# Batch 0 by pairs of heads instead of halves of heads and of slots, in a linear attention followed by two matrix products with a gelu

## Chip, cores and metric

The kernel runs on one core of a Trainium2 chip (trn2). The metric is the device time in microseconds (us) of one execution; the median of five runs counts. The profile is of one execution, and times in it run from its start.

## What is computed

Eight batches of eight heads, 576 positions, 64 elements a head. The attention is linear (no softmax), and its output goes through two matrix products with a gelu between them:

```python
def phi(x, c, s):
    r = np.maximum(x, 0.0)
    return np.concatenate([r * c, r * s], axis=-1)
q_p = phi(q, cos_w, sin_w)
k_p = phi(k, cos_w, sin_w)
kv = np.einsum('bhsf,bhsd->bhfd', k_p, v)
z = np.sum(k_p, axis=2)
num = np.einsum('bhsf,bhfd->bhsd', q_p, kv)
den = np.einsum('bhsf,bhf->bhs', q_p, z)[..., None] + 1e-06
x = num / den                      # then (B*S, H*D) = (4608, 512)
h = x @ w_in                       # w_in 512 x 2048
out = (h * (1.0 / (1.0 + np.exp(-1.702 * h)))) @ w_out    # w_out 2048 x 512
```

The sum z is had from the same matmul as kv: v has a 65th column of ones, so a numerator matmul gives 64 elements of the numerator and the denominator beside them.

## The kernel before

**Tiles.** The 4608 tokens are taken in nine blocks of 512. The first product (`mm1`, L289) gives a block's hidden values in 16 slices of 128 rows: each is four matmuls, one for each row group of 128 of x (`KC` = 4), over 512 columns, and a gelu on ScalarE (L286). The second (`mm2`, L315) multiplies them by w_out, four tiles of 128 tokens, 16 matmuls each. Batch b+1's attention is woven into block b by a table of slots (`at`, L485): what stands at slot n is issued behind slice n of the block.

**Batch 0** has nothing to hide behind and is written out by hand (L356 to L478). Its 512 first positions are four column groups ("slots") of 128; the tail of 64 positions comes later, in slot 13 of block 0 (L490). The steps, all in bf16 with f32 in PSUM:

- `prep` (L199): relu times cosine and relu times sine, for q and k, four heads at a time. Each is one instruction, on VectorE or ScalarE as `on` says.
- `turn_q0` (L360): transposes of q on TensorE, with a copy to `qT` on ScalarE, four of them.
- `kv0` (L367): k^T v, six matmuls a head, and a cast to `kvs` on ScalarE.
- `num0` (L378): eight numerator matmuls into an `at` tile: half of the heads (n) and two slots (p).
- `inv0`, `product0` (L389, L397): denominator plus eps, reciprocal, and numerator times reciprocal into `xb`, on VectorE. A group can be done slot by slot.
- `turn_x0` (L402): transposes of `xb` into a free part of the same `at` tile, and a copy into `xT` on ScalarE. A group covers two row groups (`2 * n` and the next) and two slots.
- `mm1_first` (L413): the first four slices of the first product (`first`, four PSUM tiles), in column pieces of 128, 128 and 256, as the slots come in.

**What sets the order.** The schedule is by hand: each engine does its instructions in the order of the program text, and waits by semaphores. There are two `at` tiles (two PSUM banks each) and four `mm` tiles, given out in turn, and a new user waits until the last reader of the tile is done. `warmup` (L72) issues matmuls on zeros between steps. The loads are in the order of L119 to L144, nearly all on GpSimd's queue: q and k and v of batch 0, w_in, w_out with batch 1 between, then batch 2. The tail of q of batch 0 is turned by a transposing DMA on SyncE's queue (`turn_q`, L218, called at L478), as q of batches 2 and later is.

The order of the stretch in question, cut:

```python
    kv0(kv_lo, 0, 4)
    kv0(kv_hi, 4, 6)
    na0 = num0(0, 0)
    kv0(kv_hi, 6, 8)
    product0(na0, inv0(na0), 0, 0)
...
    first = [mm_tile() for _ in range(4)]
    K4 = (0, 1, 2, 3)
    mm1_first(0, K4, 0, 128)
    turn_x0(nb0, 1, 0, (1, 2))
...
    for fc in range(4):
        mm1_first(fc, (2, 3), 256, 512)
        gelu(first[fc], fc)
```

Of the kernel before, what the change touches and what calls it, by code (L numbers as in the profile page):

```python
# [9 lines left out]
F32 = mybir.dt.float32  # L10
BF16 = mybir.dt.bfloat16
# [10 lines left out]
def kernel(  # L22
# [9 lines left out]
    nc = tc.nc  # L32
# [322 lines left out]

    prep_new(0)  # L356
    s0 = state[0]
    nums = {}
# [8 lines left out]
    def kv0(kv, h0, h1):  # L367

        v3 = s0["v"][:96].rearrange("p (j d) -> p j d", d=D)
        for h in range(h0, h1):  # L370
            for c in range(6):
                j = h * 6 + c
                nc.tensor.matmul(kv[:, ts(h % 4, 128)].rearrange("p (j d) -> p j d", j=2), kp[:96, c, h, :],  # L373
                                 v3[:, j:49:48 - j, :], start=(c == 0), stop=(c == 5))
        nc.scalar.copy(s0["kvs"][:, h0 // 4, h0 % 4:h0 % 4 + h1 - h0, 0:D + 1],
                       kv.rearrange("p (h e) -> p h e", e=128)[:, h0 % 4:h0 % 4 + h1 - h0, 0:D + 1])

    def num0(n, p):  # L378
        nm = at_tile()
        for s in range(2):  # L380
            for h in range(4):
                nc.tensor.matmul(nm[:, s, ds(h * (D + 1), D + 1)], qT[:, 4 * n + h, ts(2 * p + s, 128)],
                                 s0["kvs"][:, n, h, 0:D + 1], start=True, stop=True)
        return nm

    def nm4(nm, s0_, s1):
        return nm[:, s0_:s1, 0:4 * (D + 1)].rearrange("p s (h e) -> p s h e", e=D + 1)

    def inv0(nm, s=(0, 2)):  # L389
        k = s[1] - s[0]  # L390
        den = two.tile([128, 8], F32, name="den").rearrange("p (s h) -> p s h", s=2)[:, 0:k]
        inv = two.tile([128, 8], F32, name="inv").rearrange("p (s h) -> p s h", s=2)[:, 0:k]
        nc.vector.tensor_scalar(den, nm4(nm, *s)[:, :, :, D], 1e-6, None, op0=ADD)
        nc.vector.reciprocal(inv, den)
        return inv

    def product0(nm, inv, n, p, s=(0, 2)):  # L397
        k = s[1] - s[0]
        nc.vector.tensor_tensor(s0["xb"][:, 2 * p + s[0]:2 * p + s[1], 4 * n:4 * n + 4, :], nm4(nm, *s)[:, :, :, 0:D],
                                inv.unsqueeze(3).to_broadcast([128, k, 4, D]), op=MUL)  # L400

    def turn_x0(nm, n, p, s=(0, 2)):  # L402

        w = nm.rearrange("p b e -> p (b e)").bitcast(BF16).rearrange("p (b e) -> p b e", b=2)[:, :, 768:1024]
        for c in range(*s):
            for j in range(2):
                nc.tensor.transpose(w[:, c, ts(j, 128)], s0["xb"][:, 2 * p + c, 4 * n + 2 * j:4 * n + 2 * j + 2, :]
                                    .rearrange("p h d -> p (h d)"), ident)
        nc.scalar.copy(xT[:, 2 * n:2 * n + 2, (2 * p + s[0]) * 128:(2 * p + s[1]) * 128]  # L409
                       .rearrange("p j (s t) -> p s j t", t=128),  # L410
                       w[:, s[0]:s[1]].rearrange("p s (j t) -> p s j t", j=2))

    def mm1_first(fc, kcs, c0, c1):  # L413
        for kc in kcs:
            nc.tensor.matmul(first[fc][:, c0:c1], w_in_sb[:, kc, ts(fc, 128)], xT[:, kc, c0:c1],  # L415
                             start=(kc == 0), stop=(kc == KC - 1))
# [9 lines left out]
    prep_q0(0, 0, (VE, AC))  # L426
    prep_q0(0, 1, (VE, AC))
    for n, p in ((0, 0), (0, 1), (1, 0), (1, 1)):
        if n:
            prep_q0(n, p)  # L430
        turn_q0(n, p, AC.copy)
        if (n, p) != (1, 1):
            warmup(2)
    for n in range(2):
        for c in range(6):
            prep(0, "k", c, 4 * n, 4 * n + 4, on=(VE, AC if c > 2 else VE))
    idle = mm_tile()
    warmup(11, idle)
    kv_lo, kv_hi = mm_tile(), mm_tile()
    kv0(kv_lo, 0, 4)  # L440
    kv0(kv_hi, 4, 6)
    na0 = num0(0, 0)
    kv0(kv_hi, 6, 8)
    product0(na0, inv0(na0), 0, 0)
    warmup(2, idle)
    nb0 = num0(1, 0)
    turn_x0(na0, 0, 0)
    inv = inv0(nb0, (0, 1))
    product0(nb0, inv, 1, 0, (0, 1))
    inv = inv0(nb0, (1, 2))  # L450
    warmup(2, idle)
    na1 = num0(0, 1)
    warmup(1, idle)
    turn_x0(nb0, 1, 0, (0, 1))
    product0(nb0, inv, 1, 0, (1, 2))
    product0(na1, inv0(na1), 0, 1)
    warmup(2, idle)
    first = [mm_tile() for _ in range(4)]
    K4 = (0, 1, 2, 3)
    mm1_first(0, K4, 0, 128)  # L460
    turn_x0(nb0, 1, 0, (1, 2))
    for fc in (1, 2, 3):
        mm1_first(fc, K4, 0, 128)
    for fc in (0, 1):
        mm1_first(fc, K4, 128, 256)
    nb1 = num0(1, 1)
    turn_x0(na1, 0, 1)
    product0(nb1, inv0(nb1), 1, 1)
    for fc in (2, 3):
        mm1_first(fc, K4, 128, 256)  # L470
    for fc in range(4):
        mm1_first(fc, (0, 1), 256, 512)
    turn_x0(nb1, 1, 1)
    for fc in range(4):
        mm1_first(fc, (2, 3), 256, 512)
        gelu(first[fc], fc)
# [92 lines left out]
```

## Time and profile before

| | |
|---|---|
| median of five runs | 299.13 us (298.83 to 299.15) |
| the profiled execution: time | 299.13 us |
| its span | 297.2 us |
| instructions | 5124 |
| granted TensorE clock | 1.00 over the span |
| DMA | 39.65 MB, mean 133 GB/s |

How to read what follows. PE is TensorE's matmuls, PEld its weight loads, DVE is VectorE, ACT ScalarE, POOL GpSimd, SP SyncE. A line of a timeline has start, duration, engine, line of the kernel, operation, output and inputs, shapes and the number of instructions merged, and in brackets the idle time of the engine before it and what ended it. A line of the waits has the waiting engine and line, what it waited for, and the sum, the number and the longest of these waits. A matmul's duration holds its latency; the spacing of starts tells what it takes of TensorE.

### The profile page before, as it was taken

To read this page: it belongs to the slowest core of one execution; us is meant where nothing else is said; L and a number is where in the kernel's file an instruction comes from. 1 tells how busy PE (TensorE), PEld (TensorE's weight loads), DVE (VectorE), ACT (ScalarE), POOL (GpSimd) and SP (SyncE) were. 2 spreads that over 40 slices of the span, in tenths; PEclk is the share of its full clock that TensorE was granted. 3 is DMA by queue.
4 is the path that set the end of the run, shared out by engine and by line. 5 is a ranking of instruction groups with operands and counts; after the bars stand their busy time and mean duration, and the time that the engine had idled before them with its cause. 6 is when DMAs were issued, how large, how long until landed. Compare 5 with 4: busy or idle time off the path is not lost.

```text
span 297.2 us, 5124 instructions
## 1 busy us (share of the span) xinstructions
PE 285.8 (96%) x1956; PEld 146.8 (49%) x1992; DVE 106.1 (36%) x358; ACT 125.9 (42%) x214; POOL 97.6 (33%) x117
## 2 busy tenths in 40 slices
PE   8998999999799999999999999999999999999994
PEld 3674456555344554455445544554455444444443
DVE  5760455773490158114811482148214200000000
ACT  7827542672126512651175116511751167127411
POOL 8542270620259015800690159004501200120021
PEclk9999999999999999999999999999999999999999
DMA  7999999999979977995699969996902510011033
GB/s 188 191 204 176 201 199 193 194 137 173 187 145 175 186 115 136 184 192 99 118 186 147 166 134 185 146 156 124 187 2 60 121 42 1 35 73 35 0 70 71
DMA packets 87303, 39.65 MB, mean 133 GB/s; under 512 B 57136, under 2 KB 85040, under 8 KB 87280
## 3 DMA queue, kind: packets, MB, share of 16 engines
q0 software_dynamic: 40848, 27.01, 60.2%
q1 hardware_dynamic: 46272, 12.20, 26.3%
q8 instruction: 15, 0.25, 0.3%
q10 hardware_dynamic: 160, 0.13, 0.2%
q14 instruction: 8, 0.07, 0.1%
HBM read 36.70 MB, written 9.44 MB: 155 GB/s over the span
## 4 chain that ended last, share of the span: by engine, by line
PE 87%; DMA 5%; DVE 3%; ACT 2%; issue 1%; ACTq 0%; DVEq 0%
PE mm L281 39%; PE mm L321 37%; DMA qT<-qn 4%; PE at L265 3%; PE at L244 3%; DMA q<-in_q_dram 1%; PE mm L345 1%; DVE qn L207 1%; PE mm L415 1%; ACT g L286 1%; PE mm L373 1%; PE mm L75 1%; ACT xT L409 1%; DVE xb L273 1%; ACT qT L226 1%
## 5 line engine op out<-in xcount | busy, mean ns | idle before, releaser
L321 PE MATMUL mm<-w_out_sb,g 128*128 128x512 bf16 x543 | 126.4, 379 | 0.6
L281 PE MATMUL mm<-xT,w_in_sb 128*128 128x512 bf16 x547 | 122.7, 377 | 0.9
L333 POOL DMA_DIRECT2D out_dram<-ysb x54 | 50.6, 942 | 174.6 <-ACT ysb L331 173.1
L286 ACT ACTIVATE g<-mm 128x512 bf16<-128x512 f32 x144 | 85.6, 598 | 45.9 <-PE mm L281 44.9
L281 PEld LDWEIGHTS <-w_in_sb 128*128 128x128 bf16 x564 | 54.3, 98 | 64.1 <-issue 0.2
L321 PEld LDWEIGHTS <-g 128*128 128x128 bf16 x560 | 52.2, 98 | 57.0
L331 ACT COPY ysb<-mm 128x512 f32<-128x512 f32 x34 | 19.9, 586 | 99.8 <-PE mm L321 99.8
L248 DVE CAST kvs<-at 128x260 bf16<-128x260 f32 x14 | 5.4, 426 | 59.3 <-PE at L244 59.3
L273 DVE TENSOR_TENSOR xb<-at,inv 128x512 bf16<-128x512 f32 (+1 forms) x36 | 24.8, 689 | 1.2
L271 DVE TENSOR_SCALAR den<-at 128x8 f32<-128x8 f32 (+1 forms) x36 | 5.9, 164 | 46.0 <-PE at L265 46.0
L350 DVE COPY ysb<-mm 128x256 f32<-128x256 f32 x1 | 0.4, 425 | 59.4 <-PE mm L345 59.4
L265 PEld LDWEIGHTS <-qT 128*128 128x128 bf16 x272 | 12.9, 98 | 10.4 <-DMA qT<-qn 2.5
L207 DVE TENSOR_SCALAR qn<-q,cosw 128x512 bf16<-128x512 bf16 (+1 forms) x36 | 12.4, 349 | 12.1 <-DMA q<-in_q_dram 12.1
L265 PE MATMUL at<-kvs,qT 128*128 128x65 bf16 x272 | 14.2, 194 | 2.5 <-DMA qT<-qn 2.0
L207 DVE TENSOR_SCALAR qn<-q,sinw 128x512 bf16<-128x512 bf16 (+1 forms) x34 | 13.1, 384 | 0.0
L244 PEld LDWEIGHTS <-kp 128*128 128x128 bf16 (+1 forms) x288 | 9.6, 97 | 1.7
L244 PE MATMUL at<-vt,kp 128*128 128x65 bf16 (+1 forms) x288 | 9.8, 193 | 0.0
L86 POOL DMA_DIRECT2D v<-in_v_dram x10 | 8.3, 833 | 2.2 <-DMA w_in_sb<-in_moe_w_in_dram 2.2
L95 POOL DMA_DIRECT2D kt<-in_k_dram x6 | 8.2, 1362 | 1.9 <-DMA k<-in_k_dram 1.9
L86 POOL DMA_DIRECT2D k<-in_k_dram x9 | 7.8, 863 | 2.6 <-ACT g L286 1.9
L207 DVE TENSOR_SCALAR kp<-k,cosw 128x512 bf16<-128x512 bf16 x24 | 8.4, 350 | 0.0
L207 DVE TENSOR_SCALAR kp<-k,sinw 128x512 bf16<-128x512 bf16 x24 | 8.1, 338 | 0.0
(75 smaller groups left out, 141.8 us busy)
## 6 DMA issues: line engine op xcount, KB each, us to landing
out_dram<-ysb POOLq DMA_DIRECT2D x38, 128.0 KB, 3.0
out_dram<-ysb POOLq DMA_DIRECT2D x16, 256.0 KB, 3.0
q<-in_q_dram POOLq DMA_DIRECT2D x7, 512.0 KB, 10.4
k<-in_k_dram POOLq DMA_DIRECT2D x6, 512.0 KB, 12.0
v<-in_v_dram POOLq DMA_DIRECT2D x6, 512.0 KB, 13.0
w_out_sb<-in_moe_w_out_dram POOLq DMA_DIRECT2D x4, 512.0 KB, 19.0
w_in_sb<-in_moe_w_in_dram POOLq DMA_DIRECT2D x3, 512.0 KB, 11.9
q<-in_q_dram SPq DMA_DIRECT2D x2, 512.0 KB, 4.2
```

What stands on the lines that cost most here:

```text
L86: on.dma_start(out=state[b][n][:np_, t * D * h0:t * D * h1].rearrange("p (h e) -> p h e", h=h1 - h0), in_=SRC[n][b, h0:h1, 0:np_ * t, :].r ...
L95: on.dma_start(out=t.rearrange("p (h d) -> p h d", h=H), in_=SRC[n][b, :, 512:576, :].rearrange("h p d -> p h d"))
L207: nc.vector.tensor_scalar(oc, i, 0.0, wc, op0=MAX, op1=MUL)
L244: nc.tensor.matmul(kv[:, ds(h % 4 * (D + 1), D + 1)], kp[:r, c, h, :], vt[:r, c, h, 0:D + 1], start=(c == 0), stop=(c == last))
L265: nc.tensor.matmul(nm[:, h // 4, ds(h % 4 * (D + 1), D + 1)], q_slot(b, c)[:, h, :], state[b]["kvs"][:, h // 4, h % 4, 0:D + 1], start=Tru ...
L271: nc.vector.tensor_scalar(den[:r], nm4[:, :, :, D], 1e-6, None, op0=ADD)
L273: nc.vector.tensor_tensor(state[b]["xb"][:r, c].rearrange("p (n h) d -> p n h d", n=2), nm4[:, :, :, 0:D], inv[:r].unsqueeze(3).to_broadca ...
L281: nc.tensor.matmul(hps[:, c0:c1], w_in_sb[:, kc, ds(fc * 128, 128)], xT[:, kc, ds(i * TB + c0, c1 - c0)], start=(kc == 0), stop=(kc == KC ...
L286: nc.scalar.activation(g, hps, AF.Gelu_apprx_sigmoid)
L321: nc.tensor.matmul(yps, gT[fc][:, ds(t * 128, 128)], w_out_sb[:, fc, :], start=(fc == 0), stop=(fc == FC - 1))
L331: nc.scalar.copy(ysb, cur[t])
L333: nc.gpsimd.dma_start(out=out[row:row + (n - 1) * step + 1:step, :], in_=ysb[p0:p0 + n, :])
```

## The change

Batch 0 is done by pairs of heads (m from 0 to 3) from k^T v on. A pair is one row group of x. `kv0(m)` makes k^T v of one pair in an `mm` tile of its own, with a cast for each pair (four casts, before three). `num0(m)` makes the numerators of a pair over all four slots, eight matmuls in one `at` tile. `product0(m)` has one denominator, one reciprocal and one multiply of 512 elements a pair: four products, before five. `turn_x0(m)` does four transposes and one copy of 512 contiguous elements into `xT`'s row group m: four copies, before five. `mm1_first(kc, *fcs)` has 512-column matmuls: 16 of them, before 32 of 128 columns and 16 of 256. So the first product goes row group by row group instead of column group by column group. Four warmup matmuls fewer stand in the stretch (14 against 18 from the eleven on).

Besides, the sine part of one q relu (half 1, first pair of slots) goes from VectorE to ScalarE, whose three such relus now stand ahead of the four `qT` copies, and the sine part of one k relu goes from ScalarE to VectorE. On POOL's and SP's queues nothing is added, removed or moved.

```diff
-    def kv0(kv, h0, h1):
-
+    def kv0(m):
+
+        kv = mm_tile()
         v3 = s0["v"][:96].rearrange("p (j d) -> p j d", d=D)
-        for h in range(h0, h1):
+        for h in (2 * m, 2 * m + 1):
             for c in range(6):
                 j = h * 6 + c
-                nc.tensor.matmul(kv[:, ts(h % 4, 128)].rearrange("p (j d) -> p j d", j=2), kp[:96, c, h, :],
+                nc.tensor.matmul(kv[:, ts(h % 2, 128)].rearrange("p (j d) -> p j d", j=2), kp[:96, c, h, :],
                                  v3[:, j:49:48 - j, :], start=(c == 0), stop=(c == 5))
-        nc.scalar.copy(s0["kvs"][:, h0 // 4, h0 % 4:h0 % 4 + h1 - h0, 0:D + 1],
-                       kv.rearrange("p (h e) -> p h e", e=128)[:, h0 % 4:h0 % 4 + h1 - h0, 0:D + 1])
-
-    def num0(n, p):
-        nm = at_tile()
-        for s in range(2):
-            for h in range(4):
-                nc.tensor.matmul(nm[:, s, ds(h * (D + 1), D + 1)], qT[:, 4 * n + h, ts(2 * p + s, 128)],
-                                 s0["kvs"][:, n, h, 0:D + 1], start=True, stop=True)
-        return nm
-
-    def nm4(nm, s0_, s1):
-        return nm[:, s0_:s1, 0:4 * (D + 1)].rearrange("p s (h e) -> p s h e", e=D + 1)
-
-    def inv0(nm, s=(0, 2)):
-        k = s[1] - s[0]
-        den = two.tile([128, 8], F32, name="den").rearrange("p (s h) -> p s h", s=2)[:, 0:k]
-        inv = two.tile([128, 8], F32, name="inv").rearrange("p (s h) -> p s h", s=2)[:, 0:k]
-        nc.vector.tensor_scalar(den, nm4(nm, *s)[:, :, :, D], 1e-6, None, op0=ADD)
+        o = 2 * m % 4
+        nc.scalar.copy(s0["kvs"][:, m // 2, o:o + 2, 0:D + 1], kv[:, 0:256].rearrange("p (h e) -> p h e", e=128)[:, :, 0:D + 1])
+
+    def num0(m):
+
+        nms[m] = at_tile().rearrange("p b e -> p (b e)").rearrange("p (s e) -> p s e", s=4)
+        for s in range(4):
+            for h in range(2):
+                nc.tensor.matmul(nms[m][:, s, ds(h * (D + 1), D + 1)], qT[:, 2 * m + h, ts(s, 128)],
+                                 s0["kvs"][:, m // 2, 2 * m % 4 + h, 0:D + 1], start=True, stop=True)
+
+    def product0(m):
+        nm4 = nms[m][:, :, 0:2 * (D + 1)].rearrange("p s (h e) -> p s h e", e=D + 1)
+        den = two.tile([128, 8], F32, name="den").rearrange("p (s h) -> p s h", s=4)
+        inv = two.tile([128, 8], F32, name="inv").rearrange("p (s h) -> p s h", s=4)
+        nc.vector.tensor_scalar(den, nm4[:, :, :, D], 1e-6, None, op0=ADD)
         nc.vector.reciprocal(inv, den)
-        return inv
-
-    def product0(nm, inv, n, p, s=(0, 2)):
-        k = s[1] - s[0]
-        nc.vector.tensor_tensor(s0["xb"][:, 2 * p + s[0]:2 * p + s[1], 4 * n:4 * n + 4, :], nm4(nm, *s)[:, :, :, 0:D],
-                                inv.unsqueeze(3).to_broadcast([128, k, 4, D]), op=MUL)
-
-    def turn_x0(nm, n, p, s=(0, 2)):
-
-        w = nm.rearrange("p b e -> p (b e)").bitcast(BF16).rearrange("p (b e) -> p b e", b=2)[:, :, 768:1024]
-        for c in range(*s):
-            for j in range(2):
-                nc.tensor.transpose(w[:, c, ts(j, 128)], s0["xb"][:, 2 * p + c, 4 * n + 2 * j:4 * n + 2 * j + 2, :]
-                                    .rearrange("p h d -> p (h d)"), ident)
-        nc.scalar.copy(xT[:, 2 * n:2 * n + 2, (2 * p + s[0]) * 128:(2 * p + s[1]) * 128]
-                       .rearrange("p j (s t) -> p s j t", t=128),
-                       w[:, s[0]:s[1]].rearrange("p s (j t) -> p s j t", j=2))
-
-    def mm1_first(fc, kcs, c0, c1):
-        for kc in kcs:
-            nc.tensor.matmul(first[fc][:, c0:c1], w_in_sb[:, kc, ts(fc, 128)], xT[:, kc, c0:c1],
-                             start=(kc == 0), stop=(kc == KC - 1))
+        nc.vector.tensor_tensor(s0["xb"][:, 0:4, 2 * m:2 * m + 2, :], nm4[:, :, :, 0:D],
+                                inv.unsqueeze(3).to_broadcast([128, 4, 2, D]), op=MUL)
+
+    def turn_x0(m):
+
+        w = nms[m].rearrange("p s e -> p (s e)").bitcast(BF16).rearrange("p (s e) -> p s e", s=4)[:, :, 384:512]
+        for c in range(4):
+            nc.tensor.transpose(w[:, c], s0["xb"][:, c, 2 * m:2 * m + 2, :].rearrange("p h d -> p (h d)"), ident)
+        nc.scalar.copy(xT[:, m, 0:512].rearrange("p (s t) -> p s t", s=4), w)
+
+    def mm1_first(kc, *fcs):
+        for fc in fcs:
+            nc.tensor.matmul(first[fc], w_in_sb[:, kc, ts(fc, 128)], xT[:, kc, 0:TB], start=(kc == 0), stop=(kc == KC - 1))
 
     AC, VE = nc.scalar, nc.vector
     kvs_new(0)
@@ -423,56 +413,44 @@
         prep(0, "q", 2 * p, 4 * n, 4 * n + 4)
         prep(0, "q", 2 * p + 1, 4 * n, 4 * n + 4, on=on)
 
-    prep_q0(0, 0, (VE, AC))
-    prep_q0(0, 1, (VE, AC))
+    for n, p in ((0, 0), (0, 1), (1, 0)):
+        prep_q0(n, p, (VE, AC))
     for n, p in ((0, 0), (0, 1), (1, 0), (1, 1)):
-        if n:
+        if (n, p) == (1, 1):
             prep_q0(n, p)
         turn_q0(n, p, AC.copy)
         if (n, p) != (1, 1):
             warmup(2)
     for n in range(2):
         for c in range(6):
-            prep(0, "k", c, 4 * n, 4 * n + 4, on=(VE, AC if c > 2 else VE))
-    idle = mm_tile()
-    warmup(11, idle)
-    kv_lo, kv_hi = mm_tile(), mm_tile()
-    kv0(kv_lo, 0, 4)
-    kv0(kv_hi, 4, 6)
-    na0 = num0(0, 0)
-    kv0(kv_hi, 6, 8)
-    product0(na0, inv0(na0), 0, 0)
-    warmup(2, idle)
-    nb0 = num0(1, 0)
-    turn_x0(na0, 0, 0)
-    inv = inv0(nb0, (0, 1))
-    product0(nb0, inv, 1, 0, (0, 1))
-    inv = inv0(nb0, (1, 2))
-    warmup(2, idle)
-    na1 = num0(0, 1)
-    warmup(1, idle)
-    turn_x0(nb0, 1, 0, (0, 1))
-    product0(nb0, inv, 1, 0, (1, 2))
-    product0(na1, inv0(na1), 0, 1)
-    warmup(2, idle)
+            prep(0, "k", c, 4 * n, 4 * n + 4, on=(VE, AC if c > 2 + n else VE))
+    warmup(11, mm_tile())
+    kv0(0)
+    kv0(1)
+    num0(0)
+    kv0(2)
+    product0(0)
+    num0(1)
+    kv0(3)
+    product0(1)
+    turn_x0(0)
     first = [mm_tile() for _ in range(4)]
-    K4 = (0, 1, 2, 3)
-    mm1_first(0, K4, 0, 128)
-    turn_x0(nb0, 1, 0, (1, 2))
-    for fc in (1, 2, 3):
-        mm1_first(fc, K4, 0, 128)
-    for fc in (0, 1):
-        mm1_first(fc, K4, 128, 256)
-    nb1 = num0(1, 1)
-    turn_x0(na1, 0, 1)
-    product0(nb1, inv0(nb1), 1, 1)
-    for fc in (2, 3):
-        mm1_first(fc, K4, 128, 256)
+    warmup(3, first[0])
+    num0(2)
+    product0(2)
+    mm1_first(0, 0, 1)
+    turn_x0(1)
+    mm1_first(0, 2, 3)
+    num0(3)
+    product0(3)
+    mm1_first(1, 0, 1)
+    turn_x0(2)
+    mm1_first(1, 2, 3)
+    mm1_first(2, 0)
+    turn_x0(3)
+    mm1_first(2, 1, 2, 3)
     for fc in range(4):
-        mm1_first(fc, (0, 1), 256, 512)
-    turn_x0(nb1, 1, 1)
-    for fc in range(4):
-        mm1_first(fc, (2, 3), 256, 512)
+        mm1_first(3, fc)
         gelu(first[fc], fc)
```

More of the change, by code (lines that the diff above doesn't have):

```diff
@@ L357 @@
     s0 = state[0]
-    nums = {}
+    nms = {}
     def turn_q0(n, p, copy):
```

## Prediction

> **What bounds the kernel now.** I read the page first: busy time, then the chain that ended last.
>
> ```profile
> PE 285.8 (96%) x1956; PEld 146.8 (49%) x1992; DVE 106.1 (36%) x358; ACT 125.9 (42%) x214; POOL 97.6 (33%) x117
> ...
> PE 87%; DMA 5%; DVE 3%; ACT 2%; issue 1%; ACTq 0%; DVEq 0%
> ```
>
> TensorE is busy for 96% of the span and is 87% of the chain, so time is won only where TensorE stands still, and time won early reaches the end only if no later wait takes it back. The table of waits for PE says where it stands still after the start:
>
> ```profile
> PE at L265 <- DMA qT<-qn: 2.0, 1, 2.0
> PE at L225 <- ACT qT L226: 0.3, 1, 0.3
> ```
>
> So the change, which touches only batch 0, has to win in the first 24 us, and what it wins has to get past the one 2.0 us DMA wait. The timeline of the stretch that the diff rewrites:
>
> ```profile
> 11.85 2.27 PE L373 MATMUL mm<-v,kp 96*128 96x128 bf16 x36
> 13.95 0.42 PE L382 MATMUL at<-kvs,qT 128*128 128x65 bf16 x8
> ...
> 16.27 0.59 ACT L409 COPY xT<-at 128x512 bf16<-128x512 bf16 x1 [0.66 <-PE at L407]
> ...
> 18.86 0.69 DVE L399 TENSOR_TENSOR xb<-at,inv 128x512 bf16<-128x512 f32 x1
> ...
> 21.13 1.03 PE L415 MATMUL mm<-xT,w_in_sb 128*128 128x256 bf16 x8 [0.23 <-ACT xT L409]
> ...
> 22.42 0.59 ACT L409 COPY xT<-at 128x512 bf16<-128x512 bf16 x1 [1.34 <-PE at L407]
> 23.06 1.03 PE L415 MATMUL mm<-xT,w_in_sb 128*128 128x256 bf16 x8 [0.68 <-ACT xT L409]
> ...
> 24.12 8.79 PE L281 MATMUL mm<-xT,w_in_sb 128*128 128x512 bf16 x39
> ...
> 32.75 0.42 PE L265 MATMUL at<-kvs,qT_tail 128*128 128x65 bf16 x8
> ...
> 79.90 0.31 PEld L265 LDWEIGHTS <-qT 128*128 128x128 bf16 x8 [2.46 <-DMA qT<-qn]
> ```
>
> Start and duration are in us. From the first k^T v matmul (11.85) to the first matmul of slice 4 (24.12) 12.27 us pass. The end of this stretch is latency: PE waits for the xT copies before 21.13 and 23.06, and slice 4 waits for the first gelu (23.47 + 0.60, then 24.12).
>
> **The change, part by part.** Spacings from the records: k^T v matmuls and transposes 0.056 us each, numerators 0.0325, a 512-column matmul 0.216. From the last matmul's start to the reader's start: 0.22 + 0.04 (128 columns), 0.19 + 0.04 (numerator), 0.38 + 0.04 (512). One product, from den to the end of the multiply, is 14.41 to 15.54: 1.13. One xT copy of 512 elements is 0.59, then 0.05 until PE goes.
>
> Preparation: one q relu moves from DVE to ACT and one k relu from ACT to DVE. On DVE a q relu has a slot of 0.26, a k relu 0.20; DVE's q part ends at 8.75 instead of 9.01. On ACT the third q relu waits for the second half of q (lands at 6.00, issue plus landing time), so the first qT copy starts near 6.5 instead of 6.25; the other copies are queued behind it, but ACT idled 0.16 and 0.18 before the next two, so it is caught up by the third, and ACT then has 5 instead of 6 k relus (slot 0.40) and is free at 12.65 instead of 13.08. The last q transposes move up 0.25 and the warmup ends at 11.6; v's first heads land at 11.71, so k^T v starts at 11.77 instead of 11.85. I count that 0.08; if a copy is late it is lost.
>
> From there, with the order of the new code (m is the pair of heads):
> k^T v of pairs 0 and 1, 24 x 0.056, to 13.11. Before, 36 matmuls stood ahead of the first numerator (13.95). Pair 0's cast (0.27, ACT free at 12.65) ends at 12.95: it lies beside pair 1. Numerator 0: 13.11 to 13.37. Product 0: 13.57 to 14.70. Meanwhile k^T v of pair 2 (to 14.04), numerator 1 (14.30), k^T v of pair 3 (14.97). Product 1 follows on DVE, to 15.83. Transposes of pair 0: 14.97 to 15.19; xT copy 15.46 to 16.05, three warmups beside it.
> Numerator 2 needs pair 0's buffer, so the copy's end: 16.10 to 16.36 (before, the third group started at 16.91). Product 2: to 17.69. Two matmuls of row group 0 (16.79), transposes of pair 1 (17.01), copy 17.22 to 17.81, two matmuls beside it (17.44), wait.
> Numerator 3: 17.86 to 18.12. Product 3: 18.32 to 19.45. Two matmuls of row group 1 (18.55), transposes of pair 2 (18.77), copy 18.98 to 19.57, two matmuls (19.20), wait.
> First matmul of row group 2: 19.62 to 19.84. Transposes of pair 3: to 20.06; copy 20.27 to 20.86; three matmuls (20.71), wait.
> Row group 3 starts at 20.91; the first gelu runs from 21.33 to 21.93; slice 4 starts at 21.98. That is 24.12 - 21.98 = **2.14 us** earlier.
>
> Where it comes from: the first numerator starts 0.84 us earlier, and four products of 1.13 run beside matmuls, where before five products (three of 512 elements, two of 256) stood in DVE's queue and the last xT copy ended at 23.01, now 20.86. The first product's work on PE hardly changes: 32 x 0.056 + 16 x 0.108 = 3.5 before, 16 x 0.216 = 3.5 after. Net 4 warmups fewer, which lay in waits: nothing.
>
> A rule weighed: the Trainium skill (TensorE: Matmul & The Clock Gate, Back-to-back issue gap) gives 131 ns for a sustained 512-column matmul and 81 for a 128-column one. By it the five 512-column matmuls on the new path cost 0.43 us less. The records show 216 and 56 in this stretch, so I use those.
>
> A rule against the change: the same page (A second HAM failure mode) says that PE micro-idling often between groups of 512-column matmuls can make its clock swing between full and half. The new order has gaps of 0.20, 0.26, 0.42, 0.42 and 0.20 us between just such groups. Before has gaps of 0.40, 0.35, 0.39, 0.84 and 0.19 between 16.5 and 24.1, and the granted clock in every 2 us window there is 1.00. By the row it costs nothing; by the rule, with its window of 3.4 us at half rate, an estimated 1.7 us. I take the row, since the new gaps are shorter.
>
> **What comes late next.** Everything after 24.12 moves up, but the loads do not: up to 54.6 us the DMA engines run a backlog (busy digits of 9), whatever PE does. Issue plus landing time against use: w_in slices land at 18.7, 20.8 and 23.8 and are used from 22.0, 25.4 and 28.9: fine. The transposed q tail is issued at 22.24 and lands after 8.73, at 30.97; DVE can't start it earlier, since its q tail lands at 21.41. It is used at 32.75, which 2.14 us earlier would be 30.61. So PE waits until 31.01, and the gain is cut to **1.74 us**. The third w_out block lands at 41.90; its first use is at 43.90, now 42.16: fine by 0.26. k and v of batch 1 are ready on DVE at 40.94, used from 43.02; the fourth w_out block 44.67 against 48.4. Batch 2's data are there long before use.
>
> Then the 2.0 us wait at 79.90. Batch 2's transposes on SP start after DVE's relus, behind DVE's eviction at 55.02, which moves with PE; POOL's output stores and the loads of batch 3 move with PE too. So the wait should move as a whole. What doesn't move is the backlog until 54.6: the stores now queue behind it for longer, and some of the slack between 58 and 60 us, where the loads' queue moved only 48 KB, is lost. The loss lies between 0 (slack takes all) and 1.74 (transposes land at 79.86 as before). A loss of 0 to 0.5 is nearest to the slack of about 2 us; I take 0.2. All else up to the end follows PE.
>
> Sum: profiled execution 299.13 us (span 297.2, 1.9 around it), which is also the median of the five runs. 299.13 - 1.74 + 0.2 = **297.6 us**.
>
> **Rivals.** (a) The tail's landing doesn't bind, because it lands earlier or the front gains more: all of 2.14, 297.0. The 8.7 us landing under a full backlog speaks against it. (b) The batch 2 transposes keep their old time: the wait at 79.90 grows from 2.0 to as much as 3.7 and the gain goes back there: 298.0 to 299.1. For it: transposes landed 3.7 us apart under batch 3's loads, and 1.4 us apart later beside few loads, so they are bound by traffic. Against: that traffic is issued relative to PE. (c) Slower: the tail transpose of batch 1, issued at 56.30, now meets the stores pushed together by the backlog. In before it took 5.1 us in the slack; the next one took 6.5 us after it, when loads filled the engines, and the later ones 3.7. If the tail is starved likewise, the whole row of transposes, and with it the numerator at 79.90, is late by 6.5 - 3.7 = 2.8 us: 299.13 - 1.74 + 2.8 = 300.2. It decides against the change once the row is delayed by over 1.74. (d) The clock swings: 299.13 - 2.14 + 1.7 = 298.7, and 300.4 if for two windows. (e) The front doesn't do what it says, because the ACT queue (relus, casts, copies in one line) is late at each copy: each 0.1 us at the four copies costs 0.1 on the path, and 0.4 only uses up what the tail's landing cuts off anyway.
>
> **How the numbers follow.** Likeliest, with (e)'s small slips inside, 55%: 297.4 to 298.0, so 297.6. (a) 10%: 296.9 to 297.3. (b) 20%: 298.0 to 299.1, half of it within 0.2% (0.6 us, about what a measurement of this kernel can tell from no change). (c) 9%. (d) and larger slips 6%, two thirds of it within 0.2%. Faster 0.55 + 0.10 + 0.10 = 0.75; same 0.10 + 0.04 = 0.14; slower 0.09 + 0.02 = 0.11. The range 296.9 to 298.9 leaves out the slower cases and the worst of (b).
>
> **What would show it.** In the changed profile: first numerator near 13.1; numerators 2 and 3 ended by xT copies near 16.1 and 17.9; slice 4 near 22.0; a wait of about 0.4 us for the q tail near 31.0; the first matmul of w_out's third block near 42.2; the transposes' wait still about 2 us, now at 78. I am wrong if slice 4 starts after 22.6, if the granted clock falls under 1.00 between 16 and 24 us, or if the numerator after the transposes' wait still starts near 79.9.

## The result and the profile after

The changed kernel takes 296.65 us, the median of 31 runs (295.85 to 298.34), beside 298.89 us for the kernel before in 52 runs (297.2 to 302.65). The ratio is 0.9932, with a 95% interval of 0.9918 to 0.9945, so the gain is 1.6 to 2.5 us. The prediction was 297.6 us with a range of 296.9 to 298.9: the sign was right, and the time lies 0.25 us under the range. As a gain, 1.5 us were forecast, with a range of 0.2 to 2.2, and 2.24 measured; a quarter of a microsecond of the miss in time is that the forecast was counted from 299.13 us, one set of five runs, where 52 runs give 298.89. The profiled execution took 296.59 us with a span of 294.6 us, 2.54 us less than the profiled one of before. In the later series some runs of the kernel before took about 301 us, nearly all of them at a mean granted clock of 0.991 to 0.994 where the others had 0.997 to 1.00, so ratios there lie a few tenths of a per cent lower than here, and times of variants are therefore compared with one another too.

From the page of the changed kernel, the busy time and the chain that ended last:

```profile
PE 284.8 (97%) x1920; PEld 144.4 (49%) x1956; DVE 105.8 (36%) x355; ACT 125.9 (43%) x214; POOL 94.8 (32%) x117
...
PE 89%; DMA 5%; ACT 2%; DVE 2%; issue 1%; ACTq 0%; DVEq 0%
```

TensorE did 1.0 us less work (four warmups of 0.216 us fewer are most of it), so the other 1.5 us came out of its waits. Where they went is in the timeline of the rewritten stretch (start, duration, engine, line, operation, and in brackets the idle time before it):

```profile
13.30 0.41 PE L385 MATMUL at<-kvs,qT 128*128 128x65 bf16 x8
...
15.57 0.59 ACT L402 COPY xT<-at 128x512 bf16<-128x512 bf16 x1
...
16.21 0.41 PE L385 MATMUL at<-kvs,qT 128*128 128x65 bf16 x8
...
17.95 0.41 PE L385 MATMUL at<-kvs,qT 128*128 128x65 bf16 x8 [0.24 <-ACT xT L402]
...
19.68 0.38 PE L406 MATMUL mm<-xT,w_in_sb 128*128 128x512 bf16 x1 [0.24 <-ACT xT L402]
...
20.32 0.59 ACT L402 COPY xT<-at 128x512 bf16<-128x512 bf16 x1 [0.69 <-PE at L401]
...
22.02 1.24 PE L281 MATMUL mm<-xT,w_in_sb 128*128 128x512 bf16 x5
```

The chain is as the prediction laid it out: numerators 2 and 3 and row group 2 each start when an xT copy ends, four copies make the pace, and slice 4 starts at 22.02 (predicted 21.98). Measured from the first k^T v matmul (11.84) that is 10.18 us, before 12.27.

What came late next is where the prediction failed. From the timeline of TensorE behind slice 4:

```profile
30.64 0.42 PE L265 MATMUL at<-kvs,qT_tail 128*128 128x65 bf16 x8
...
74.23 0.43 PE L265 MATMUL at<-kvs,qT 128*128 128x65 bf16 x8 [0.39 <-DMA qT<-qn]
...
77.34 0.43 PE L265 MATMUL at<-kvs,qT 128*128 128x65 bf16 x8 [0.95 <-DMA qT<-qn]
```

and the table of waits of TensorE (sum, number, longest):

```profile
PE at L265 <- DMA qT<-qn: 1.3, 2, 1.0
```

The tail's numerator at 30.64 has no bracket: no wait. And the wait for batch 2's transposes, 1.97 us in before, is now 0.39 + 0.95 = 1.34: it shrank by 0.63 where 0.2 was to be lost. By terms: 299.13 - 2.10 (front) - 0.63 (that wait) = 296.40 against the 296.59 of the profiled run; 0.19 stays unexplained.

### The profile page after: what moved, and what is told of

Read it like the earlier page. It is cut to its first block, busy times and chain, and to the rows that moved or that the text cites. A ratio compares the mean times of both kernels' runs of the same rounds, so it can differ in the third digit from the quotient of the medians.

```text
span 294.6 us, 5047 instructions
## 1 busy us (share of the span) xinstructions
PE 284.8 (97%) x1920; PEld 144.4 (49%) x1956; DVE 105.8 (36%) x355; ACT 125.9 (43%) x214; POOL 94.8 (32%) x117
## 3 DMA queue, kind: packets, MB, share of 16 engines
q0 software_dynamic: 40848, 27.01, 59.5%
## 4 chain that ended last, share of the span: by engine, by line
PE 89%; DMA 5%; ACT 2%; DVE 2%; issue 1%; ACTq 0%; DVEq 0%
PE mm L281 39%; PE mm L321 37%; DMA qT<-qn 4%; PE at L265 3%; PE at L244 3%; DMA q<-in_q_dram 1%; PE mm L345 1%; ACT g L286 1%; PE mm L75 1%; PE mm L406 1%; PE mm L375 1%; PE mm L365 1%; DVE xb L273 1%; ACT qT L226 1%; PE at L385 0%
## 5 line engine op out<-in xcount | busy, mean ns | idle before, releaser
L273 DVE TENSOR_TENSOR xb<-at,inv 128x512 bf16<-128x512 f32 (+1 forms) x36 | 24.8, 689 | 1.2
L86 POOL DMA_DIRECT2D v<-in_v_dram x10 | 9.2, 929 | 5.1 <-PE at L225 2.6
L272 DVE RECIPROCAL inv<-den 128x8 f32<-128x8 f32 (+1 forms) x36 | 7.2, 201 | 1.2
```

What stands on the lines that cost most here:

```text
L86: on.dma_start(out=state[b][n][:np_, t * D * h0:t * D * h1].rearrange("p (h e) -> p h e", h=h1 - h0), in_=SRC[n][b, h0:h1, 0:np_ * t, :].r ...
L272: nc.vector.reciprocal(inv[:r], den[:r])
L273: nc.vector.tensor_tensor(state[b]["xb"][:r, c].rearrange("p (n h) d -> p n h d", n=2), nm4[:, :, :, 0:D], inv[:r].unsqueeze(3).to_broadca ...
```

## The experiments

All times are medians of each kernel's own runs (number in brackets), and the ratio is to the kernel before on the same chip. "Front" is from the first k^T v matmul to slice 4, "tail" is from the issue of the tail's transpose to its landing, "batch 2" the sum of TensorE's waits for that batch's transposes.

| kernel | us (runs) | ratio, 95% interval | front | tail | batch 2 |
|---|---|---|---|---|---|
| before | 298.89 (52) | | 12.27 | 8.7 | 2.0 |
| before again | 298.77 (18) | 0.9946 to 1.0002 | 12.18 | 8.6 | 1.8 |
| changed | 296.65 (31) | 0.9918 to 0.9945 | 10.18 | 7.9 | 1.3 |
| changed again | 296.58 (6) | 0.9847 to 0.9937 | 10.09 | 7.9 | 1.4 |
| relus back | 296.57 (6) | 0.9842 to 0.9930 | 10.15 | 7.7 | 1.4 |
| ten warmups ahead of slice 4 | 298.46 (22) | 0.9940 to 0.9985 | 12.13 | 7.9 | 1.2 |
| kv0(2) ahead of num0(0) | 296.86 (6) | 0.9902 to 0.9948 | 10.64 | 7.9 | 1.3 |
| tail used in slot 11 | 297.65 (15) | 0.9917 to 0.9973 | 10.05 | 7.9 | 1.0 |
| pair 1 turned early | 296.78 (12) | 0.9868 to 0.9932 | 9.18 | 7.9 | 3.0 |
| ... and tail in slot 15 | 296.66 (6) | 0.9837 to 0.9931 | 9.07 | 7.9 | 2.6 |
| ... and w_out's third block ahead of v | 295.94 (6) | 0.9811 to 0.9909 | 9.20 | 7.8 | 1.4 |
| before with 24 more PE instructions | 300.25 (22) | 0.9996 to 1.0035 | 12.18 | 8.0 | 2.9 |
| changed with 36 more | 295.99 (9) | 0.9880 to 0.9940 | 10.06 | 8.5 | 0 |
| ... and tail in slot 15 | 295.79 (6) | 0.9834 to 0.9910 | 10.15 | 8.5 | 0.8 |
| all of it, 36 more | 296.15 (6) | 0.9842 to 0.9923 | 9.16 | 8.6 | 0.8 |
| all of it, 24 more | 296.51 (6) | 0.9850 to 0.9943 | 9.18 | 9.0 | 1.8 |
| loads of batch 3 later | 296.57 (6) | 0.9896 to 0.9951 | 10.06 | 7.9 | 1.1 |

My theory was that the front is worth what it was predicted to be, and that the tail's landing, taken from before, was too late. The rivals were that the front gives more than its 2.1 us, that the moved relus carry part of it, and that the gain comes from the transposes of batch 2 instead.

**Do the readings repeat?** The changed kernel again (with nothing edited):

> The changed kernel once more, for the spread of what my forecast took from one profile. Theory A (the front gained what I worked out, 2.1 us, and reaches the end whole; the q tail's landing, 30.97 in before and 30.20 in after, only spreads from run to run, so the cut to 1.74 was one profile's landing): slice 4 at 22.0 again, the tail lands anywhere between 30.0 and 31.1, and the ratio to before is 0.993 within 0.001. Theory B (the changed order itself makes the tail land earlier): it lands at 30.2 within 0.15.

Measured: k^T v at 11.58, slice 4 at 21.67, tail from 21.97 to 29.89, batch 2's waits 0.38 + 1.06. So the start moves by 0.3 us from run to run, with the first loads; the front, the tail's 7.9 us and the shrunken wait repeat. And before again, likewise unedited:

> The kernel before, profiled once more, for where its q tail lands. In the profile of before the tail landed 19.1 us after the first k^T v matmul; in the changed kernel and three variants of it 18.3 to 18.7. Theory A (the 19.1 was one draw of a spread): 18.2 to 19.2 here, and the later loads shifted along. Theory B (the changed order brings it forward): 19.1 within 0.15.

Measured: slice 4 at 24.28, tail from 22.69 to 31.32, a wait of 1.82 us at 79.91. The tail's 8.6 to 8.7 us belong to before, and 7.9 to the changed kernel.

**The moved relus.** In the changed kernel both go back to where they were:

```diff
-    for n, p in ((0, 0), (0, 1), (1, 0)):
+    for n, p in ((0, 0), (0, 1)):
...
-        if (n, p) == (1, 1):
+        if n:
...
-            prep(0, "k", c, 4 * n, 4 * n + 4, on=(VE, AC if c > 2 + n else VE))
+            prep(0, "k", c, 4 * n, 4 * n + 4, on=(VE, AC if c > 2 else VE))
```

> The changed kernel with the two relus put back as before: q's on DVE, k's on ACT. ACT then does 6 k relus, so the first cast moves from 12.83 to near 13.1 and the first numerator from 13.3 to near 13.4; product 0 then ends at 15.0, when PE is free for its transposes anyway. Theory A (the gain is the order by pairs): 0 to 0.1 us slower than the changed kernel, ratio 0.993 to 0.9935. Rival C (the relus carry part of the gain, through the ACT queue): 0.3 us slower or more.

Measured: 296.57 us, front 10.15. Its profile had k late (k^T v only at 12.53, with a 0.5 us wait on VectorE's `kp`), and the median is nevertheless that of the changed kernel. The relus carry nothing that can be measured; the 0.08 us counted for them can be neither seen nor excluded.

**Does the front's gain reach the end?** Give it back behind the front, as ten warmups:

```diff
         gelu(first[fc], fc)
+    warmup(10)
     prep(0, "q", 4)
```

> The changed kernel with ten warmup matmuls of 0.216 us (2.16 us of TensorE) ahead of slice 4; the front is as changed. Theory A (every us at the front reaches the end one for one, nothing behind it takes it up in this range): the time of before, ratio to before 1.000 within 0.003, and the tail still lands 18.2 to 19.2 us after the first k^T v matmul. Theory B (the tail lands earlier because PE is earlier): it lands later again, near 19.1. Rival C (only part of the front's time reaches the end, the rest of the gain is from elsewhere): ratio 0.996 or less.

The timeline of TensorE there:

```profile
21.62 2.32 PE L75 MATMUL at<-warm 128*128 128x512 bf16 x9
23.78 1.46 PE L281 MATMUL mm<-xT,w_in_sb 128*128 128x512 bf16 x6
```

The front is 12.13 us instead of 10.09 in the repeat of the changed kernel, 2.04 longer, and the time 298.46 - 296.58 = 1.88 longer (the two sets ran on different chips). So the front's time reaches the end nearly one for one. Theory A's ratio of 1.000 within 0.003 was missed, though: it is 0.9963, so a changed kernel with the front of before is still faster than before, by 0.3 to 0.4 us between the medians and by 1.1 by the ratio on its own chip. That part is not the front's; in the profile, batch 2's wait is 1.2 us here beside 2.0 in before. The tail took 7.9 us here too, with slice 4 nearly as late as in before. So a late slice 4 isn't what makes the tail take 8.7.

A second edit moves the front by a smaller, known step, pair 2's k^T v back ahead of the first numerator:

```diff
     kv0(1)
-    num0(0)
     kv0(2)
+    num0(0)
     product0(0)
```

> The changed kernel with k^T v of pair 2 ahead of numerator 0 instead of behind it, so that the first numerator again follows 36 matmuls as in before. If the front is a chain of latencies from the first numerator on: product 0, the first xT copy and numerator 2 are later by 0.5 us and slice 4 with them (22.5), time 296.6 plus 0.4 to 0.6. If TensorE's work sets the front: no change.

Measured: front 10.64 instead of 10.18, and 296.86 us, 0.2 to 0.3 more than the three sets of runs of the changed kernel, where 0.4 to 0.6 were expected. The 0.46 is seen in the front; the rise of the time is too small beside the scatter to say how much of it reaches the end.

**What the tail's landing costs.** Use it two slots earlier:

```diff
-                at(13, unit_num, 0, 4)
-                at(13, turn_x, 0, 4)
+                at(11, unit_num, 0, 4)
+                at(11, turn_x, 0, 4)
```

> The changed kernel with the numerator of the q tail in slot 11 instead of 13, so that PE asks for the tail at about 28.9. Theory A (the tail lands near 30 to 31 whatever PE does): PE waits there for 1.1 to 2.1 us, which is lost to the end, so the time comes back to between 297.7 and 298.8, ratio 0.996 to 1.000. Rival D (the tail's landing follows PE, or a wait there is taken up later): ratio stays at 0.993.

The waits of TensorE:

```profile
PE at L265 <- DMA qT_tail<-qn: 1.7, 1, 1.7
PE at L265 <- DMA qT<-qn: 1.0, 1, 1.0
```

A wait of 1.66 us at 30.37, which ends with the landing at 30.32, costs 1.07 us (297.65 - 296.58), a little less than theory A's 1.1 to 2.1; the wait of batch 2 takes part of it back. So a tail that lands late would have cost most of its lateness, as the prediction had it. In the changed kernel it lands at 30.20, 0.44 ahead of its use, and cuts nothing off.

**Why does it land earlier?** It is issued at 22.30 (before 22.24), so the flight is what differs. A table of half-microsecond windows shows the flight in before (the columns are window, TensorE, weight loads, VectorE, ScalarE, GpSimd in us busy with counts, granted clock, DMA share, GB/s):

```profile
27.00:27.50 0.50, 0.50 (x4) 0.22 (x3) 0.00 (x0) 0.50 (x1) 0.46 (x1) 1.00 1.80 183
27.50:28.00 0.50, 0.50 (x4) 0.20 (x2) 0.00 (x0) 0.23 (x2) 0.00 (x0) 1.00 2.63 45
28.00:28.50 0.50, 0.50 (x4) 0.26 (x3) 0.00 (x0) 0.37 (x1) 0.00 (x0) 1.00 0.09 10
28.50:29.00 0.50, 0.50 (x4) 0.23 (x3) 0.00 (x0) 0.36 (x1) 0.00 (x0) 1.00 1.03 163
```

and in the changed kernel:

```profile
27.50:28.00 0.50, 0.50 (x4) 0.20 (x3) 0.00 (x0) 0.49 (x1) 0.22 (x1) 1.00 1.25 193
28.00:28.50 0.50, 0.50 (x5) 0.21 (x3) 0.00 (x0) 0.24 (x1) 0.00 (x0) 1.00 1.27 189
```

In before, all 16 DMA engines together move 45 and 10 GB/s between 27.5 and 28.5, beside 189 and 193 in the changed kernel: about 0.8 us in which the traffic stands still, the same 0.8 by which the tail takes longer. What precedes it is in the list of DMA queues (packets, MB, share) from 26.5 to 27.5 us, of before:

```profile
q0 software_dynamic: 144, 0.15, 112.7%
q1 hardware_dynamic: 144, 0.04, 35.0%
q8 instruction: 1, 0.02, 5.8%
```

and of the changed kernel in the same window:

```profile
q0 software_dynamic: 149, 0.15, 89.4%
q1 hardware_dynamic: 153, 0.04, 29.6%
```

q1 holds the transpose's small packets, q8 loads instructions. The page counts 15 packets and 0.25 MB on q8, 16 KB each. It has 1956 + 1992 = 3948 records of TensorE's matmuls and weight loads before and 1920 + 1956 = 3876 after; if the packets are TensorE's, one is about 260 of its instructions, and with 72 fewer every later load comes 72 instructions later in the work. In the changed kernel the load comes at 31.0, after the tail has landed. The theory: an instruction load for TensorE that falls into a transposing DMA's flight is followed by a standstill of the DMA traffic of 0.7 to 1 us. The rival: the standstill comes from the order of the loads and their timing against TensorE's work. To tell them apart, change the number of instructions alone. In the kernel before, four of the twelve opening warmups (zeros, ahead of any data) are cut in four pieces of 128 columns, 512 columns as before, but 24 instructions more:

```diff
-    warmup(12)
+    wps = at_tile()[:, 0]
+    warmup(8, wps)
+    for _ in range(16):
+        nc.tensor.matmul(wps[:, 0:128], warm[:, 0:128], warm[:, 0:128], start=True, stop=True)
```

> The kernel before, with four of the twelve opening warmup matmuls cut into four of 128 columns each: the same TensorE time, 24 more instructions on PE's queue, nothing else. In both profiles of before a 16 KB instruction load (queue q8) falls at 26.8 to 27.0, while the q tail's transposing DMA is in flight, all DMA traffic stands still for 0.8 us right after it, and the tail takes 8.6 to 8.7 us from issue to landing; in the changed kernel, with 72 instructions fewer, the load falls at 31.0 and the tail takes 7.7 to 7.9. Theory F (the instruction load during a DMA transpose stops the traffic): here the load falls near 24.3, before the transposing begins, and the tail takes 7.9 us. Rival G (the tail's time is set by something else that the change moved): 8.65 us as before. The whole time: within 0.3% of before, since the tail is not late there.

Its DMA queues from 24.5 to 25 us:

```profile
q0 software_dynamic: 103, 0.10, 122.3%
q8 instruction: 1, 0.02, 11.7%
```

and its windows, with the columns as above:

```profile
27.50:28.00 0.50, 0.50 (x4) 0.22 (x3) 0.00 (x0) 0.23 (x2) 0.50 (x1) 1.00 1.23 191
28.00:28.50 0.50, 0.50 (x4) 0.27 (x3) 0.00 (x0) 0.50 (x1) 0.24 (x1) 1.00 1.29 188
```

The load has moved to 24.8, when no transpose packet is moving yet (no q1), the standstill is gone, and the tail takes 8.0 us from an issue at 22.77, with slice 4 at 24.30 as in before. The reverse, in the changed kernel, puts a load into the flight: the same edit with `warmup(6, wps)` and `range(24)`, 36 instructions more.

> The changed kernel with six of the opening warmups cut in four each: the same TensorE time, 36 more instructions on PE. Theory F: the instruction load moves from 31.0 to about 27.1, into the tail's flight; the traffic stands still for 0.8 us near 28, the tail takes 8.6 us or more and lands near 31.0, where PE asks for it at 30.6, so 0.3 to 0.4 us are lost there as my forecast had it; time 296.6 plus 0.3, plus or minus what the later loads' new places do at batch 2's transposes. Rival G: the tail takes 7.9 us and the time is that of the changed kernel.

Its queues from 27.5 to 28 us:

```profile
q1 hardware_dynamic: 84, 0.02, 32.1%
q8 instruction: 1, 0.02, 12.0%
```

its windows:

```profile
28.50:29.00 0.50, 0.50 (x4) 0.20 (x2) 0.00 (x0) 0.24 (x1) 0.00 (x0) 1.00 2.86 77
29.00:29.50 0.50, 0.50 (x4) 0.24 (x3) 0.00 (x0) 0.50 (x1) 0.00 (x0) 1.00 0.25 32
29.50:30.00 0.50, 0.50 (x4) 0.24 (x3) 0.00 (x0) 0.23 (x2) 0.00 (x0) 1.00 1.34 185
```

and the timeline of TensorE at the tail's use:

```profile
31.48 0.43 PE L265 MATMUL at<-kvs,qT_tail 128*128 128x65 bf16 x8 [0.79 <-DMA qT_tail<-qn]
```

The load at 27.7, the standstill a microsecond later, the tail 8.5 us from an issue at 22.88, and a wait of 0.79 us at 31.5: the wait that the prediction had expected of the changed kernel. So both directions hold, with the same work on TensorE: the place of the instruction load makes the tail's landing. The rival falls. All 17 traces, one for each row of the table, agree: in the six in which a load comes among the tail's transpose packets (at 26.8 to 28.7 us) the tail takes 8.5 to 9.0 us, in the eleven others 7.7 to 8.0.

But the time doesn't follow. The kernel of before with the tail mended is not faster (300.25 us, ratio 0.9996 to 1.0035), and the changed kernel with the tail spoiled is not slower (295.99, against 296.57 in runs of the unchanged work on the same chip; the intervals of the two ratios overlap, so that it's faster isn't sure). The later loads moved too, and with them batch 2's transposes: the waits there are 0.95 + 1.96 = 2.9 us in the one (the fourth transpose lands at 81.15, in before at 79.86) and gone in the other (76.72). A mended 0.8 us at the tail was not on the path in before, where the tail lands at 30.97 and is used at 32.75; batch 2's wait is on it.

**Batch 2's row of transposes.** The same question can be put to the traces of batch 2: do transpose packets (q1) move when the load comes? In before there is a load at 76.96 us, with 500 such packets between 76.5 and 77.5, and the traffic stands still just ahead of the fourth landing at 79.86:

```profile
78.50:79.00 0.50, 0.00 (x0) 0.00 (x0) 0.00 (x0) 0.10 (x1) 0.10 (x1) 1.00 0.05 5
79.00:79.50 0.50, 0.00 (x0) 0.00 (x0) 0.00 (x0) 0.00 (x0) 0.50 (x2) 1.00 0.08 10
```

There the fourth transpose lands 4.56 us after the third, in the changed kernel 3.11: its load at 78.44 comes after the fourth has landed at 77.30. But the changed kernel has a standstill earlier in the row, at 64.5 to 65.5, after a load at 63.3. The three kernels with 36 more instructions (two of them follow below) have none between 62 us and the fourth landing. Their load comes at 58.1 to 59.3, when hardly a transpose packet moves. The queues of the changed kernel from 63 to 63.5 us:

```profile
q1 hardware_dynamic: 156, 0.04, 68.0%
q8 instruction: 1, 0.02, 17.6%
```

and of the first kernel with 36 more from 59 to 59.5:

```profile
q8 instruction: 1, 0.02, 12.0%
q1 hardware_dynamic: 9, 0.00, 2.6%
```

From the first transpose's issue to the fourth's landing these three take 20.4 to 21.4 us, the changed kernel 21.8, before 22.2, and all kernels with a standstill in between 21.3 to 23.4. That fits the theory, but no run moves this load alone. Not every lull is of this kind, either: traffic also falls without a load (56.5 to 57.5 and 82.5 to 83.5 in the changed kernel), and the lull at 58.8 to 60.0 in before follows a load at 57.2 with no transpose packet moving.

**Is more to be had from the front?** Three edits, each on top of the other. First, pair 1's transposes go ahead of numerator 2, and the matmuls of the first product behind them:

```diff
-    warmup(3, first[0])
+    warmup(2, first[0])
+    turn_x0(1)
     num0(2)
...
     mm1_first(0, 0, 1)
-    turn_x0(1)
-    mm1_first(0, 2, 3)
     num0(3)
     product0(3)
-    mm1_first(1, 0, 1)
+    mm1_first(0, 2, 3)
+    mm1_first(1, 0)
     turn_x0(2)
```

> The changed kernel with the transposes of pair 1 ahead of numerator 2, in the place of one warmup, and the rest of the front drawn up behind: slice 4 should start at 21.1 instead of 22.0. Theory A (the front's latency is the bound, but the q tail lands at 30.2 to 31 by itself): PE asks for the tail at 29.7 and waits 0.5 to 1.2 us, so of the 0.9 us gained between 0 and 0.4 reaches the end; ratio 0.992 to 0.993. Rival D (nothing cuts it off): all 0.9, ratio 0.990.

Its waits of TensorE:

```profile
PE at L265 <- DMA qT<-qn: 3.0, 2, 1.5
...
PE at L265 <- DMA qT_tail<-qn: 0.3, 1, 0.3
```

The front is 9.18 us, 0.9 to 1.0 shorter, and the time is 296.78: nothing gained. 0.35 goes at the tail, and the wait of batch 2 grows from 1.3 to 3.0 us. This is rival (b) of the prediction, one microsecond further on. Second, the tail's use moves from slot 13 to 15 (`at(13, ...)` becomes `at(15, ...)` in the two lines of the edit to slot 11):

> The front drawn up by 0.9 us as in the run before (transposes of pair 1 early), and the q tail's numerator moved from slot 13 to slot 15, so that PE asks for the tail 1.7 us later and it is no longer late. Theory A (the loads pace PE next): the third w_out block, which lands at 41.3 to 41.5 in the same profiles, is now asked for at about 40.9, so PE waits there 0.4 to 0.6 us; 0.3 to 0.5 of the 0.9 us remains; ratio 0.991 to 0.993. Rival D (only the tail cut it off): ratio 0.990.

Its waits of TensorE, in which the tail's is gone:

```profile
PE at L265 <- DMA qT<-qn: 2.6, 2, 1.6
PE mm L321 <- DMA w_out_sb<-in_moe_w_out_dram: 0.7, 1, 0.7
```

Another has come: 0.66 us at 41.52 for w_out's third block, which lands at 41.47; and batch 2's are 2.6. Time 296.66. Third, that block is loaded ahead of v of batch 1:

```diff
-    for n in "qkv":
+    for n in "qk":
         load_main(1, n)
     load_w_out(2)
+    load_main(1, "v")
     load_w_out(3)
...
-            k0, k1, ks = (11, 24, (25, 26, 27, 28)) if i == 0 else (0, 12, (17, 19, 21, 23, 25))
+            k0, k1, ks = (11, 25, (26, 27, 28, 29)) if i == 0 else (0, 12, (17, 19, 21, 23, 25))
```

> As the last one, and the third w_out block is loaded ahead of v of batch 1, with k^T v of batch 1 and its numerators one slot later. Theory A: no load is late in block 0, so all 0.9 us gets as far as block 1: 0.9 us under the changed kernel (about 295.7), ratio 0.990. If batch 2's transposes keep their old time the wait near 77 us grows by what was won and nothing reaches the end: ratio 0.993.

Now no load is waited for in block 0, batch 2's wait is 1.4 us, and the time 295.94, the first that is below the changed kernel's (its profiled run started late, k^T v at 12.67; the ratio's interval overlaps the changed kernel's).

**The two together.** The changed kernel with 36 more instructions and the tail in slot 15, so that neither the tail nor batch 2 should be waited for:

> The changed kernel with the 36 more instructions on PE as in the run before last, and the q tail's numerator in slot 15. In that run the standstill in the tail's flight cost PE a wait of 0.79 us at slot 13, and batch 2's waits were gone. Theory F: asked for 1.7 us later, the tail is no longer late, and nothing else changes: 0.5 to 0.8 us below that run (295.9), so 295.1 to 295.4. Rival H (another load is late in its place, the third w_out block at 41.5 to 42.3): 295.7 or more.

It missed: 295.79 us. The number is rival H's, but no wait for w_out is in the table of waits, which has this instead:

```profile
PE at L265 <- DMA qT<-qn: 0.8, 1, 0.8
```

The tail's 0.79 us is won, but TensorE now stands 0.81 us at 76.68 for batch 2's fourth transpose, landed at 76.64 (76.72 in the kernel that waited at the tail). It comes no earlier, although TensorE does. The faster front and moved load with 36 and with 24 more instructions:

> The front drawn up by 0.9 us, the tail in slot 15, the third w_out block ahead of v of batch 1 (295.9 when last run, with a wait of 1.4 us at batch 2's transposes), and the 36 more instructions. Theory F: the instruction load leaves the flight of batch 2's transposes, as it did in the changed kernel with these instructions, and that wait goes: 294.5 to 295.0. If the transposes are bound by the loads of batch 3 alone, the wait stays: 295.9.

> The same with 24 more instructions in place of 36, so that the instruction load falls 2.6 us of matmuls later, near 61 to 62 us, nearer to the flight of batch 2's first transposes. Theory F: between the run with 36 and the one with none, 294.8 to 295.9, with a wait at batch 2's transposes whenever a standstill falls in their flight before the fourth has landed. If only the amount of work counts, it equals the other two.

Both missed in time: 296.15 and 296.51 us. With 36, TensorE waits 0.55 us at 43.38 for the next batch's data and 0.81 at 76.58 (landing 76.54); with 24, a load comes at 61.6, a standstill at 62.5 to 63.5, and the wait is 1.79 us at 75.17. So in three kernels with 36 more instructions and fronts from 9.16 to 10.15 us the fourth transpose lands at 76.5 to 76.7. In these three a faster front doesn't move it; why it stays there isn't shown.

**Loads of batch 3.** An edit that was to issue them later, in slot 8 of block 1, on the changed kernel:

```diff
-                at(1, load_all, b + 1)
+                at(8 if i == 1 else 1, load_all, b + 1)
```

> The changed kernel with the loads of batch 3 issued behind slice 8 of block 1 instead of slice 1, so that batch 2's transposes do not share the DMA engines with them at first. If the traffic of the loads sets the transposes' pace (3.7 us each), they land in time, the waits near 74 and 77 us (1.3 us in the profile of the changed kernel) go, and the time is 1.0 to 1.4 us shorter, near 295.4. If the standstills after instruction loads set it, or the loads then collide with what follows: less than 0.4 us either way.

Inconclusive: GpSimd has nothing else in its queue between the two places, so the loads go out at the same times (v of batch 3 at 57.58), and the kernel is a repeat of the changed one, 296.57 us. Whether batch 2's transposes come earlier beside less traffic stays open.

## Why the prediction missed its range

- **The front: right.** 2.14 us were forecast, 2.10 measured in the profile; numerators 2 and 3 were put at 16.10 and 17.86 and started at 16.21 and 17.95, slice 4 at 21.98 and 22.02. (The first numerator was 0.19 late, at 13.30 for 13.11; the copies behind it made up most of that.) Giving it back costs 1.88 us of 2.04. The 0.08 us for the relus can't be told from nothing.
- **The clock: right.** The row was taken against the skill's rule on micro-idling. Counted as the prediction counts them, from 0.216 us after the last 512-column matmul's start to the next start, the two largest gaps came out at 0.41 us (put at 0.42); the brackets of the timeline count from the modelled end and say 0.24. The granted clock is 1.00 in every 2 us window from 16 to 24 us and over the whole span. The rule's 1.7 us don't appear in this case.
- **The tail: the step that failed first.** "It is issued at 22.24 and lands after 8.73, at 30.97; DVE can't start it earlier" cut the gain to 1.74. The start was right (22.30), but the 8.73 us of flight were taken over from before as a property of the backlog. 0.8 of them are a standstill after an instruction load that, with 72 instructions fewer, no longer falls into the flight. It took 7.9, landed at 30.20, and cost 0 instead of 0.4. This was rival (a), given 10% because "the 8.7 us landing under a full backlog speaks against it"; the backlog is as full in the changed kernel (189 and 193 GB/s), and the landing is earlier.
- **Batch 2's wait: the larger miss.** "I take 0.2" as a loss, with bounds from 0 to 1.74: it was a gain of 0.63 (wait 1.34 instead of 1.97, the fourth transpose 77.30 instead of 79.86, so 2.56 earlier while TensorE was 2.1 earlier). The bound was drawn at zero without a reason that excluded a gain. That instruction count alone moves this wait is shown (2.0 to 2.9 in one kernel, 1.3 to 0 in another). By which path is shown only in part: the missing standstill is a likely cause of the gain with 36 more, but before and the changed kernel have one each ahead of the fourth landing, and why the row of transposes is 0.46 us shorter in the changed kernel stays open, and with it most of the 0.63. So this half of the cause stays open.
- **Rival (b), the old time of the transposes,** did not come at 2.1 us of gain but does beyond it: 0.9 us more front gave nothing by itself.
- **The range.** Both misses go the same way, 0.40 + 0.83 = 1.23 us, less the 0.04 by which the front's gain was smaller, less the 0.19 unexplained: 297.6 - 1.0 = 296.6, the profiled time. None of the prediction's three signs of being wrong appeared: they watched the front, the clock and a wait that grows, and both misses were waits that shrank.

## What to carry to other kernels

A landing time read from one trace is not a constant of the load: here 0.8 of 8.7 us depended on where TensorE's instruction loads fell. If a change alters the number of TensorE's instructions, look at which flights of transposing DMAs the loads fall into, and give waits on transposing DMAs a range on both sides of zero. And when a front is made shorter, measure what is late next in steps: 2.1 us came through nearly whole here, the next 0.9 not at all.

## What the runs showed that was not expected

- **An instruction load that stops the data.** The Trainium skill (Runtime: NRT & Kernel Launch, Instruction fetch mechanics) says that the sequencer fetches blocks of 16 KiB, 256 instructions, on a DMA queue of its own, and that crossing a block's end is mostly hidden. The size agrees (15 packets, 0.25 MB), and TensorE's table of waits has none for it. But when the load came while a transpose's packets moved, the core's DMA traffic fell to 10 to 80 GB/s for about 0.8 us, roughly a microsecond later, in before twice and in the changed kernel with 36 instructions more. Up to 81 us of all 17 traces there are 34 such loads, with 42 or more q1 packets in the microsecond ahead, and each is followed within 2.5 us by half a microsecond at 24 GB/s or less; later in the traces some are followed only by a dip, to 69 to 119. Loads with no transpose packet moving (at 31.0 us in the changed kernel, at 24.8, ahead of the tail's first packet at 26.7, in before with 24 more) were followed by none. Nor were the 8 KB loads on q14 at 86.8 to 91.4 us, which came amid over 700 transpose packets: the traffic stays at 96 GB/s or more. What in the load stops the traffic isn't shown.
- **Time without work.** 24 or 36 more instructions for the same columns on TensorE moved the span of the profiled run from 297.2 to 298.5 us in before and from 294.6 to 294.0 in the changed kernel; by the intervals of the ratios neither is sure, so changes under 1 us in this kernel may be no more than a matter of where loads fall.
- **The best version measured** has 295.79 us (changed, 36 more instructions, tail in slot 15; ratio 0.9834 to 0.9910), 295.94 with the earlier transposes and w_out's third block ahead of v. Both are faster than before; against the changed kernel's 296.65 their intervals overlap.
